# A filter-and-MLP kernel on one core: pieces 6 and 7 of the weight conversion moved to before the filter's first block, ScalarE's share of a piece one step later, and the last pieces spread over other quads

## The chip, the cores and the metric

The kernel runs on one core of a Trainium2 chip. The metric is the time on the device in microseconds (us), the median of several executions. One core has TensorE (PE in the profile; PEld is its weight load), VectorE (DVE), ScalarE (ACT), GpSimd (POOL) and SyncE (SP). Each works through its own instructions in order and waits for others by semaphores. SP does nothing here but issue DMA transfers; POOL issues others, and a few come from ScalarE.

## The reference

```
X = rfft(x, axis=1)                      # x: 8 x 3008 x 256, float32
Y = X * (filt_r + 1j * filt_i)           # filter: 1505 x 256
y = irfft(Y, n=3008, axis=1)             # 8 x 3008 x 256
h = y.reshape(24064, 256) @ w_in         # w_in: 256 x 2048
g = where(h > 0, h, exp(min(h, 0)) - 1)
out = g @ w_out                          # w_out: 2048 x 256
```

The two weight matrices arrive as float64, as pairs of 32-bit words, and the kernel turns them into float32 on the chip.

## The kernel before

**The transform.** 3008 is 47 times 64. Of each of the 8 batches, the forward transform first applies a factor of length 64 (six chunks c of four residues each, `a_first` for batch 0, `x_unit` and `a_unit` for the others) and then, in eight blocks g of the spectrum, a factor of length 47, called the second factor here (`b_unit`). `b_unit` also multiplies by the filter: eight matmuls into two PSUM tiles `psr` and `psi`, then four DVE instructions (L309 to L312). `bi_unit` takes the block back through the length 47 (matmuls into `pva` and `pvb`, two copies on ACT, L329 and L330), `y_write` puts it into DRAM, `y_read` reads it back in another layout, and `n_unit` applies the last factor (matmuls L360, two copies L362, four adds of DVE L383 to L386 that prepare the operands of the product with `w_in`). In what follows B(g) is `b_unit` of batch 0 and block g, and I(g) is `bi_unit` of the same.

**The MLP.** Its work is a list of items (batch b, sixth m of the rows, quarter q of the 2048 columns), 192 in all. One step i of the loop at the end of the kernel is called a quad here: it issues the product with `w_in` of item i ("up") and the product with `w_out` of item i-1 ("down"). Both are done as seven matrix products of half size with sums before and after them (Strassen's scheme in Winograd's form), each product being four matmuls of PE: L408 for up, into PSUM tiles phs, pha and phd, L490 for down, into po. ACT copies up results (L419) and computes the exponential part in two instructions (L425, L426), DVE adds (L416), joins (L430) and forms the sums for the way down (L466 to L470). phs is one tile that three copies read in turn, so PE's next matmuls into it wait for the copy before. Item 0 has no way down beside it, so in quad 0 PE has up work alone.

**The order of the work** is written by hand: each engine executes its instructions as they are issued in the program. In a quad it is

```
for k in "UUDUDDU": ...          # four up products, three down products
for fn, a in plan.get((i, 0)):   # place 0 of quad i
for k in "DUUDUDD": ...          # the other three up and four down products
up_tail(); down_tail()
for fn, a in plan.get((i, 1)):   # place 1 of quad i
```

`plan` holds the rest of the work, put there with `at(quad, place, function, arguments)`: the transform of the next batch, loads, outputs. In quads 0 to 3 this includes the conversion of the last weight piece, `x_unit` and `a_unit` of batch 1, and (quad 1, place 1) `n_unit(0, 1)`.

**The weight conversion.** A piece k (0 to 15, four to each quarter q: two of `w_in`, two of `w_out`) is 128 by 512 numbers. `w_fetch(k)` loads it (512 KB, one transfer for a piece of `w_in`, two for one of `w_out`; L564). `w_split` is two DVE instructions on the upper word (L576, L577: mantissa and exponent). `w_float` is four instructions of ACT (L582: lower word to float; L583: mantissa to float; L586 and L587: exponent to a power of two). `w_join` is DVE again (L593, L595, then L600 or two of L606). After each second piece `w_sums` adds four DVE instructions (L614 to L617) that form the sums of the weights. `step(k)` in the program is split and float of piece k and then the join of piece k-1. There are two sets of temporary tiles, used by even and odd pieces in turn.

**The opening phase**, before the quads: SP's queue carries x, the transform's tables and some pieces; POOL's queue carries the first pieces, then rearranges the filter in DRAM (`f_arrange`, L623 to L636, into `fd`), then reads it in eight blocks (`f_read`, L292, into `ff`), with pieces 10 to 15 in between and behind. A fetch needs its buffer: pieces 6 to 9 are loaded into the buffers of the x chunks 0 to 3 once `a_first` has read them. `a_first(c)` is 16 matmuls (L250) in two halves with eight copies by ACT (L257); `x_load_first(c)` loads its rows in two transfers (L238, L239) and, for c = 2 and 4, the table of two chunks (L243). `t_first(g)` transposes block g on PE (L269) and copies it with ACT (L270, two per block) into a tile whose buffer, for blocks 6 and 7, is that of blocks 4 and 5, so that this copy waits for the matmuls of B(4) and B(5). B(g) uses the same two PSUM tiles for every g from 1 on, and I(g) the other two: B(g+1) on PE waits for the product g on DVE, and I(g+1) for the copies of I(g) on ACT.

In the phase of the second factor, step g of the loop issues `t_first(g + 2)` (g from 2 to 5), I(g-2), B(g), the write of block g-2, and then, for g below 6, `step(g + 6)`: pieces 6 to 11 are converted there, pieces 0 to 5 before it, 12 to 14 after it, and 15 in quads 0 to 2.

Of the kernel before, what the change touches and what calls it, by code (L numbers as in the profile page):

```python
# [33 lines left out]
NXC = H // XC  # L34
# [79 lines left out]
def kernel(  # L114
# [9 lines left out]
    nc = tc.nc  # L124
# [446 lines left out]
    def w_split(k):  # L571
        m, e, c = wtmp[k % 2 if k < 15 else 0]
        f, l = c[:, 0], c[:, 1]
        wts[k] = m, e, f, l
        hi = wds[k][:, :, 1]
        nc.vector.tensor_scalar(out=m, in0=hi, scalar1=0x000FFFFF, scalar2=None, op0=ALU.bitwise_and)  # L576
        nc.vector.tensor_scalar(out=e, in0=hi, scalar1=0x7FF00000, scalar2=None, op0=ALU.bitwise_and)  # L577

    def w_float(k):
        m, e, f, l = wts[k]  # L580

        nc.scalar.activation(out=l, in_=wds[k][:, :, 0], func=AXT.Identity, scale=2.0 ** -52)  # L582
        nc.scalar.activation(out=f, in_=m, func=AXT.Identity, scale=2.0 ** -20, bias=1.0)  # L583

        ef = e.bitcast(FP32)
        nc.scalar.activation(out=ef, in_=e, func=AXT.Relu, scale=-8.0, bias=edges[:, 0:1])  # L586
        nc.scalar.activation(out=e, in_=ef, func=AXT.Relu, scale=-1.0, bias=edges[:, 1:2])  # L587
# [50 lines left out]
    with tc.manual_schedule():  # L638


        with tc.tile_pool(name="boot", bufs=1) as bp:
            ff = bp.tile([P, NG, 2, 2, D], FP32, name="ff")
            once = bp.tile([P, 2, P], FP32, name="once")
            eye, gf = once[:, 0], once[:, 1].rearrange("p (v q) -> p v q", v=2)
            pq = [bp.tile([P, 2, D], FP32, name="pq%d" % i) for i in range(2)]
            zt[0] += [bp.tile([P, 16 * ROWS], FP32, name="zt%d" % i) for i in range(2)]

            for z in zt[0] + zt[1]:
                nc.gpsimd.memset(z.rearrange("p (k r) -> p k r", r=ROWS)[:, :, 48:64], 0.0)
            for k in (1, 2, 3):  # L650
                w_fetch(k)
            f_arrange()
            w_fetch(0, nc.sync)
            for c in range(NXC):
                x_place_first(c)
            for c in range(3):
                x_load_first(c)
            w_fetch(4, nc.sync)
            nc.scalar.memzero(ff[:, 0:NG // 2])
            nc.vector.memset(ff[:, NG // 2:NG], 0.0)  # L660
            wtmp.append([kp.tile([P, 512], U32, tag=t, name=n) for t, n in (("k0", "wm"), ("k1", "we"))] +
                        [kp.tile([P, 2, 512], FP32, tag="c", name="wfl")])
            wtmp.append([sdp.tile([P, 2, D], FP32, tag="sd", name=n).bitcast(U32).rearrange("p a b -> p (a b)")
                         for n in ("wm", "we")] +
                        [t1p.tile([P, XC, D], FP32, tag="t1", name="wfl").rearrange("p (a b) d -> p a (b d)", a=2)])
            for i, v in enumerate((1151.0 * 2 ** 23, 255.0 * 2 ** 23)):
                nc.vector.memset(edges[:, i:i + 1], v)

            def step(k):
                w_split(k)  # L670
                w_float(k)
                if k > 0:
                    w_join(k - 1)

            for k in range(3):
                step(k)
            w_fetch(5, nc.sync)
            for c in range(3, NXC):
                x_load_first(c)
            nc.sync.dma_start(once, once_d)  # L680
            nc.sync.dma_start(gs, gs_d)
            a_first(0)
            w_fetch(6, nc.sync)
            step(3)
            for c in (1, 2):
                a_first(c)
                w_fetch(c + 6, nc.sync)
            step(4)
            a_first(3)
            w_fetch(9, nc.sync)  # L690
            step(5)
            for c in (4, 5):
                a_first(c)
            tn_read(0, 0)
            for g in range(NG):
                f_read(0, g, ff[:, g])
                if 3 <= g < 5:
                    w_fetch(g + 7)
            for k in (12, 13):
                w_fetch(k)  # L700
            for g in range(4):
                t_first(g)
            for g in range(NG + 2):
                if 2 <= g < NG - 2:
                    t_first(g + 2)
                if g >= 2:
                    bi_unit(0, g - 2)
                if g < NG:
                    b_unit(0, g, ff[:, g], gf, pq if g % 2 else None)
                if g >= 2:  # L710
                    y_write(0, g - 2, (nc.sync, nc.scalar if g == NG + 1 else nc.sync))
                if g < 6:
                    step(g + 6)
                    if g == 0:
                        w_fetch(14)
                if g == 7:
                    w_join(11)
                    w_split(12)
            w_float(12)
            y_read(0, 0, (nc.sync, nc.scalar))  # L720
            step(13)
            w_fetch(15)
            step(14)
        w_join(14)
        for c in range(2):
            x_load(1, c)
        yp = pool("yp", 2)
        gp = pool("gp", 2)
        ep = pool("ep", 2)
        op = pool("op", 1)  # L730
        n_unit(0, 0)

        PER = 24
        plan = {}

        def at(quad, place, fn, *a):
            plan.setdefault((quad, place), []).append((fn, a))


        for quad, place, fn in ((0, 0, w_split), (0, 1, w_float), (1, 1, w_join), (2, 1, w_sums)):
            at(quad, place, fn, 15)
        for c in range(2, XBUFS):
            at(c - 2, 0, x_load, 1, c)
        for i, f in enumerate(fbufs):
            at(3 + i, 1, nc.vector.memset, f, 0.0)
        for b in range(B):
            t = (b - 1) * PER
            if b > 0:  # L750
                for c, s in enumerate((1 if b == 1 else 0, 2, 3, 4, 6, 7)):
                    at(t + s - 1, 0, x_unit, b, c)
                    at(t + s, 0, a_unit, b, c)
                    nb, nxt = (b, c + XBUFS) if c + XBUFS < NXC else (b + 1, c + XBUFS - NXC)
                    if nb < B:
                        at(t + s, 0, x_load, nb, nxt)
                    at(t + s, 0, z_write, b, c)
                for g in range(NG + 2):
                    s = t + 9 + g
                    if g >= 2:  # L760
                        at(s, 1, bi_unit, b, g - 2)
                    if g < NG:
                        at(s, 1, b_unit, b, g)
                    if g >= 2:
                        at(s, 1, y_write, b, g - 2)
                for g in range(NG):
                    s = t + 7 + g
                    at(s, 1, f_read, b, g)
                    at(s, 1, z_read, b, g)
            for m, (s, place) in enumerate(((20, 0), (25, 1), (29, 1), (32, 0), (36, 0), (40, 0))):  # L770
                if b > 0 or m > 0:
                    at(t + s - (1 if m == 0 else 2), 0, tn_read, b, m)
                    at(t + s - (1 if m == 0 else 2), 0, y_read, b, m)
                    at(t + s, place, n_unit, b, m)
                at(t + PER + 4 * m + 5, 0, c_unit, b, m)
                at(t + PER + 4 * m + 6, 0, o_unit, b, m)

        items = [(b, m, q) for b in range(B) for m in range(6) for q in range(4)]
        for i in range(-PER, len(items) + 3):
            ups, up_tail = up_steps(*items[i]) if 0 <= i < len(items) else ((), None)  # L780
            downs, down_tail = down_steps(*items[i - 1]) if 1 <= i <= len(items) else ((), None)
            ups, downs = list(ups), list(downs)
            for k in "UUDUDDU":
                s = ups if k == "U" else downs
                if s:
                    s.pop(0)()
            for fn, a in plan.get((i, 0), ()):
                fn(*a)
            for k in "DUUDUDD":
                s = ups if k == "U" else downs  # L790
                if s:
                    s.pop(0)()
            if up_tail:
                up_tail()
            if down_tail:
                down_tail()
            for fn, a in plan.get((i, 1), ()):
                fn(*a)
# [32 lines left out]
```

## Time and profile before

| | us |
|---|---|
| median of 6 runs | 2655.39 |
| fastest and slowest of them | 2653.61, 2656.33 |
| the profiled execution's own time | 2656.33 |
| its span, first to last instruction | 2654.5 |
| busy: PE, DVE, ACT, POOL | 2601.7, 1843.8, 1509.1, 236.8 |
| first matmul of a quad (L408) | 106.71 |
| first product with the filter on DVE (L309) | 49.61 |

The mean granted clock of TensorE is 0.990 of full speed. Of the chain of work that ended last, followed back from the last instruction, 97% is PE, 43% of the span in the down products of L490. In rows of a timeline the first number is the start in us from the beginning of the span, the second the duration (or, where several are merged, the time from the first start to the last end), and in brackets at the end stands the time that the engine was idle before the instruction and what released it. DMA shares are the mean busy share of the core's 16 DMA engines. An issue row of SP or POOL is only the time to put a transfer into its queue, not the transfer.

### The profile page before, as it was taken

The page shows a single profiled execution, that of the slowest core. Times are in us where ns is not written, and L with a number is a line of the kernel's source. Part 1 is how long each engine was busy: PE and PEld are TensorE (multiplying, and loading weights), DVE is VectorE, ACT ScalarE, POOL GpSimd, SP SyncE. Part 2 cuts the span into 40 slices and gives each one's busy share as a digit, 9 for nine tenths or more (in the row PEclk, how much of TensorE's full clock was granted, in tenths as well). Part 3 has the DMA queues.
Part 4 walks back from the last instruction along what each step waited for, and adds up shares of the span by engine and source line. Part 5 has one row for each costly group of instructions (what it writes and reads, how often), then busy time and mean ns, then how long its engine had stood idle before and what let it go on. Part 6 is the DMA issues. An engine that isn't in the chain of part 4 may idle for free.

```text
span 2654.5 us, 37333 instructions
## 1 busy us (share of the span) xinstructions
PE 2601.7 (98%) x13508; PEld 2215.6 (83%) x13508; DVE 1843.8 (69%) x3203; ACT 1509.1 (57%) x2622; POOL 236.8 (9%) x298
## 2 busy tenths in 40 slices
PE   5799999999999999999999999999999999999998
PEld 4488789887898878988789878898789887899887
DVE  5776766677666776667767676676767677666666
ACT  6655555555555555655556555565555655555554
POOL 5001200011000210002100021001210011000000
PEclk8899999999999999999999999999999999999999
DMA  9534311533134322333214342134321333110010
GB/s 281 137 89 106 97 39 43 119 89 86 33 80 109 75 76 50 95 75 93 69 38 103 80 105 61 39 88 106 96 53 39 76 81 85 38 40 19 21 28 17
DMA packets 224456, 202.85 MB, mean 76 GB/s; under 512 B 127586, under 2 KB 191090, under 8 KB 224272
## 3 DMA queue, kind: packets, MB, share of 16 engines
q1 hardware_dynamic: 211632, 166.70, 25.3%
q0 software_dynamic: 11184, 33.04, 4.9%
q8 instruction: 107, 1.75, 0.3%
q10 hardware_dynamic: 1456, 0.72, 0.1%
q14 instruction: 77, 0.63, 0.1%
HBM read 128.52 MB, written 74.97 MB: 77 GB/s over the span
## 4 chain that ended last, share of the span: by engine, by line
PE 97%; DMA 2%; DVE 1%; ACT 0%; issue 0%; SPq 0%; POOL 0%; DVEq 0%; ACTq 0%; POOLq 0%
PE po L490 43%; PE phs L408 25%; PE phd L408 12%; PE pha L408 6%; PE psn L360 3%; PE pva L297 2%; PE psr L297 2%; PE psa L209 2%; DMA xc<-in_x_dram 1%; PE psa L250 0%; PE pvb L297 0%; DMA ff<-fd 0%; DMA f<-in_moe_w_out_dram 0%; PE po L269 0%; PE psi L297 0%
## 5 line engine op out<-in xcount | busy, mean ns | idle before, releaser
L490 PE MATMUL po<-g,wo 128*128 128x256 f32 (+1 forms) x5376 | 1298.2, 376 | 0.0
L490 PEld LDWEIGHTS po<-g,wo 128*128 128x128 f32 x5376 | 1016.2, 190 | 129.8 <-issue 15.8
L419 ACT ACTIVATE g<-phs 128x512 f32<-128x512 f32 (+1 forms) x576 | 339.1, 589 | 846.7 <-PE phs L408 846.0
L416 DVE TENSOR_TENSOR g<-phd,g 128x512 f32<-128x512 f32 (+1 forms) x384 | 259.6, 676 | 461.6 <-ACT e L426 277.7
L426 ACT ACTIVATE e<-e 128x512 f32<-128x512 f32 (+1 forms) x768 | 477.5, 622 | 24.4
L408 PE MATMUL phs<-y,wi 128*128 128x256 f32 (+1 forms) x1536 | 395.6, 380 | 0.0
L408 PE MATMUL phs<-ys,wi 128*128 128x256 f32 (+1 forms) x1536 | 389.1, 376 | 4.0 <-ACT g L419 4.0
L430 DVE SCALAR_TENSOR_TENSOR g<-e,g 128x512 f32<-128x512 f32 (+1 forms) x576 | 387.2, 672 | 0.2 <-ACT e L426 0.2
L425 ACT ACTIVATE e<-g 128x512 f32<-128x512 f32 (+1 forms) x576 | 352.9, 613 | 32.6 <-DVE g L416 28.0
L408 PEld LDWEIGHTS phs<-y,wi 128*128 128x128 f32 x1536 | 285.1, 190 | 83.2 <-ACT t L329 34.1
L408 PEld LDWEIGHTS phs<-ys,wi 128*128 128x128 f32 x1536 | 292.6, 191 | 37.9 <-ACT g L419 4.7
L430 DVE SCALAR_TENSOR_TENSOR g<-e,phs 128x512 f32<-128x512 f32 (+1 forms) x192 | 130.0, 677 | 139.7 <-ACT e L426 139.7
L408 PE MATMUL pha<-y,wi 128*128 128x256 f32 (+1 forms) x768 | 194.2, 375 | 0.0
L425 ACT ACTIVATE e<-phs 128x512 f32<-128x512 f32 (+1 forms) x192 | 113.0, 589 | 142.3 <-PE phs L408 141.5
L408 PE MATMUL phd<-ys,wi 128*128 128x256 f32 (+1 forms) x768 | 193.8, 375 | 0.0
L408 PE MATMUL phd<-y,wi 128*128 128x256 f32 (+1 forms) x768 | 193.7, 375 | 0.0
L318 POOL TENSOR_TENSOR sr<-sr,sp 128x512 f32<-128x512 f32 x56 | 71.2, 1271 | 1246.3 <-DVE sp L311 1246.3
L408 PEld LDWEIGHTS pha<-y,wi 128*128 128x128 f32 x768 | 146.4, 191 | 16.7
L408 PEld LDWEIGHTS phd<-ys,wi 128*128 128x128 f32 x768 | 145.7, 190 | 16.7 <-DVE g L416 0.2
L408 PEld LDWEIGHTS phd<-y,wi 128*128 128x128 f32 x768 | 145.8, 190 | 16.5
L467 DVE TENSOR_TENSOR g<-g,g 128x512 f32<-128x512 f32 (+1 forms) x192 | 130.7, 681 | 6.7
L470 DVE TENSOR_TENSOR g<-g,g 128x512 f32<-128x512 f32 (+1 forms) x192 | 130.7, 681 | 6.6
(133 smaller groups left out, 2384.1 us busy)
## 6 DMA issues: line engine op xcount, KB each, us to landing
yd<-t SPq DMA_DIRECT2D x127, 192.0 KB
t<-yd SPq DMA_DIRECT2D x190, 128.0 KB
z<-t SPq DMA_DIRECT2D x84, 256.0 KB
f<-fd POOLq DMA_DIRECT2D x112, 192.0 KB, 3.6
t<-z SPq DMA_DIRECT2D x224, 96.0 KB
out_dram<-o SPq DMA_DIRECT2D x632, 32.0 KB
tn<-tn_t SPq DMA_DIRECT2D x48, 256.0 KB
xc<-in_x_dram SPq DMA_DIRECT2D x84, 128.0 KB
```

Source lines behind the costliest of these rows:

```text
L297: nc.tensor.matmul(ps[:, u:u + w, :], table[k, v, :], r[k, u:u + w, :], start=n == 0, stop=n == len(rhs) - 1)
L318: nc.gpsimd.tensor_tensor(out=sr, in0=sr, in1=p, op=ALU.add)
L360: nc.tensor.matmul(ps[:, ts(q, P)], t[:, i - 4 * m, ds(dh * P, P)], w[:, i - 4 * m, :], start=True, stop=True)
L408: nc.tensor.matmul(ps[:, a, 0:h], w_in[q][:, COMBO[n], a, :], y[n], start=start and a == 0, stop=True, skip_group_check=True)
L416: nc.vector.tensor_tensor(out=g[o], in0=i0, in1=i1, op=ALU.add)
L419: nc.scalar.activation(out=g[o], in_=i0, func=AXT.Copy)
L425: nc.scalar.activation(out=e, in_=src, func=AXT.Relu, scale=-1.0)
L426: nc.scalar.activation(out=e, in_=e, func=AXT.Exp, scale=-1.0)
L430: nc.vector.scalar_tensor_tensor(out=g[n], in0=es[n], scalar=1.0, in1=src, op0=ALU.subtract, op1=ALU.max)
L467: nc.vector.tensor_tensor(out=b12, in0=b22, in1=b12, op=ALU.subtract)
L470: nc.vector.tensor_tensor(out=g["t4"], in0=g["b21"], in1=g["t2"], op=ALU.subtract)
L490: nc.tensor.matmul(po[i][:, u, 0:h], w_out[q][:, COMBO[n], a, :], g[n][:, a, :], start=q == 0 and a == 0 and n in (1, 3, 6, 4), stop=True, ...
```

## The change

Pieces 6 and 7: `step(6)` moves from behind B(0) to before `a_first(4)`, and the split of 7 and the join of 6 to before the transposes of the first blocks. For this the fetch of piece 6 moves up on SP's queue, ahead of the rows of x chunk 5 and of the tables `once` (with the identity for the transposes) and `gs`. In the phase of the second factor, four steps remain in place of six: after B(g), for g from 0 to 3, DVE joins piece g+7 and splits piece g+8, and ACT's four instructions for piece g+7 (g from 0 to 4) are issued between I(g-2) and B(g). Piece 14 is fetched with 12 and 13; POOL's queue keeps its order. Behind the phase, piece 13 is split with 12, and the order of DVE's work on pieces 12 to 14 is the same as before but for the join of 14, which now comes after the adds of `n_unit(0, 0)`. Piece 15: split in quad 0 as before, ACT's instructions no longer behind quad 0 but two behind quad 1 and two in the middle of quad 2, the join behind quad 2 instead of quad 1, the sums in the middle of quad 3 instead of behind quad 2. The number of instructions of every kind is unchanged.

```diff
--- before.py
+++ after.py
@@ -576,11 +576,17 @@
         nc.vector.tensor_scalar(out=m, in0=hi, scalar1=0x000FFFFF, scalar2=None, op0=ALU.bitwise_and)
         nc.vector.tensor_scalar(out=e, in0=hi, scalar1=0x7FF00000, scalar2=None, op0=ALU.bitwise_and)
 
-    def w_float(k):
+    def w_float(k, part=None):
         m, e, f, l = wts[k]
+        if part == 1:
+            return w_power(e)
 
         nc.scalar.activation(out=l, in_=wds[k][:, :, 0], func=AXT.Identity, scale=2.0 ** -52)
         nc.scalar.activation(out=f, in_=m, func=AXT.Identity, scale=2.0 ** -20, bias=1.0)
+        if part is None:
+            w_power(e)
+
+    def w_power(e):
 
         ef = e.bitcast(FP32)
         nc.scalar.activation(out=ef, in_=e, func=AXT.Relu, scale=-8.0, bias=edges[:, 0:1])
@@ -675,12 +681,13 @@
             for k in range(3):
                 step(k)
             w_fetch(5, nc.sync)
-            for c in range(3, NXC):
+            for c in (3, 4):
                 x_load_first(c)
+            a_first(0)
+            w_fetch(6, nc.sync)
+            x_load_first(5)
             nc.sync.dma_start(once, once_d)
             nc.sync.dma_start(gs, gs_d)
-            a_first(0)
-            w_fetch(6, nc.sync)
             step(3)
             for c in (1, 2):
                 a_first(c)
@@ -689,6 +696,7 @@
             a_first(3)
             w_fetch(9, nc.sync)
             step(5)
+            step(6)
             for c in (4, 5):
                 a_first(c)
             tn_read(0, 0)
@@ -696,8 +704,10 @@
                 f_read(0, g, ff[:, g])
                 if 3 <= g < 5:
                     w_fetch(g + 7)
-            for k in (12, 13):
+            for k in (12, 13, 14):
                 w_fetch(k)
+            w_split(7)
+            w_join(6)
             for g in range(4):
                 t_first(g)
             for g in range(NG + 2):
@@ -705,23 +715,27 @@
                     t_first(g + 2)
                 if g >= 2:
                     bi_unit(0, g - 2)
+                if g < 5:
+                    w_float(g + 7)
                 if g < NG:
                     b_unit(0, g, ff[:, g], gf, pq if g % 2 else None)
                 if g >= 2:
                     y_write(0, g - 2, (nc.sync, nc.scalar if g == NG + 1 else nc.sync))
-                if g < 6:
-                    step(g + 6)
-                    if g == 0:
-                        w_fetch(14)
+                if g < 4:
+                    w_join(g + 7)
+                    w_split(g + 8)
                 if g == 7:
                     w_join(11)
                     w_split(12)
+                    w_split(13)
             w_float(12)
             y_read(0, 0, (nc.sync, nc.scalar))
-            step(13)
+            w_float(13)
+            w_join(12)
             w_fetch(15)
-            step(14)
-        w_join(14)
+            w_split(14)
+            w_join(13)
+            w_float(14)
         for c in range(2):
             x_load(1, c)
         yp = pool("yp", 2)
@@ -729,6 +743,7 @@
         ep = pool("ep", 2)
         op = pool("op", 1)
         n_unit(0, 0)
+        w_join(14)
 
 
 
@@ -739,8 +754,9 @@
             plan.setdefault((quad, place), []).append((fn, a))
 
 
-        for quad, place, fn in ((0, 0, w_split), (0, 1, w_float), (1, 1, w_join), (2, 1, w_sums)):
-            at(quad, place, fn, 15)
+        for quad, place, fn, *a in ((0, 0, w_split, 15), (1, 1, w_float, 15, 0), (2, 0, w_float, 15, 1), (2, 1, w_join, 15),
+                                    (3, 0, w_sums, 15)):
+            at(quad, place, fn, *a)
         for c in range(2, XBUFS):
             at(c - 2, 0, x_load, 1, c)
         for i, f in enumerate(fbufs):
```

## The prediction

> **What bounds the kernel now.** First the busy time of each engine by stretch (columns: the stretch, then busy us and instruction count of PE, PEld, DVE, ACT, POOL, then granted clock, DMA share, GB/s).
>
> ```profile
> 120.00:125.00 5.00, 4.74 (x13) 4.30 (x14) 1.91 (x3) 0.75 (x2) 0.00 (x0) 0.50 0.00 1
> 125.00:130.00 5.00, 5.00 (x34) 3.93 (x33) 0.61 (x2) 2.56 (x5) 0.00 (x0) 0.86 0.19 56
> 130.00:230.00 100.00, 100.00 (x560) 88.95 (x559) 73.02 (x132) 59.48 (x105) 2.58 (x5) 1.00 0.42 104
> 230.00:2630.00 2400.00, 2400.00 (x12417) 2053.75 (x12415) 1672.93 (x2885) 1362.93 (x2363) 198.93 (x225) 1.00 0.28 69
> ```
>
> From 130 us on PE is busy for all of 100 and all of 2400 us at clock 1.00: nothing there can be hidden or uncovered unless PE stands still, and whatever PE starts earlier ends earlier, one for one. So the change is worth what it does to the first 126 us, plus any new hole in PE. There are two places.
>
> The first is the opening phase. The VectorE and SyncE timelines (start, duration, engine, line, tiles, then idle time before and its releaser):
>
> ```profile
> 32.44 0.69 DVE L600 TENSOR_TENSOR wi<-wfl,we 128x512 f32<-128x512 f32 x1
> 49.61 0.69 DVE L309 TENSOR_TENSOR sr<-psr,ff 128x512 f32<-128x512 f32 x1 [16.47 <-PE po L269]
> ```
> ```profile
> 24.33 0.48 SPq L238 DMA_DIRECT2D x<-in_x_dram  x1
> 26.05 0.61 SPq L239 DMA_DIRECT2D x<-in_x_dram  x1
> ...
> 31.46 5.26 SPq L564 DMA_DIRECT2D wd<-in_moe_w_out_dram  x4
> 37.77 1.60 SPq L564 DMA_DIRECT2D wd<-in_moe_w_in_dram  x2
> 39.41 0.42 SPq L342 DMA_DIRECT2D tn<-tn_t  x1
> ```
>
> DVE stands 16.47 us until the first filter block `ff` is in. The fetch of piece 6 (first of the four at 31.46) is issued so late because SP's transfers use eight semaphores in turn: each issue waits until the transfer eight before it has landed. So a landing is read off as the issue eight places later: x rows of chunk 3 are issued at 17.86 and let 31.46 go; chunk 4's table lets the fourth go at 36.4; chunk 5's two halves landed at 37.8 and 39.0. From 49.61 DVE works without a gap until 84.9. Then:
>
> ```profile
> 79.86 0.68 DVE L309 TENSOR_TENSOR sr<-psr,ff 128x512 f32<-128x512 f32 x1
> 86.23 0.69 DVE L309 TENSOR_TENSOR sr<-psr,ff 128x512 f32<-128x512 f32 x1 [1.22 <-PE psi L297]
> 89.98 0.69 DVE L309 TENSOR_TENSOR sr<-psr,ff 128x512 f32<-128x512 f32 x1 [1.26 <-PE psi L297]
> ```
> ```profile
> 72.28 0.72 ACT L587 ACTIVATE we<-we,edges 128x512 uint32<-128x512 f32 x1
> 72.91 1.06 ACT L270 ACTIVATE t<-po 112x512 f32<-112x512 f32 x2
> 73.87 0.60 ACT L329 ACTIVATE t<-pva 128x512 f32<-128x512 f32 x1
> 79.58 1.08 ACT L270 ACTIVATE t<-po 112x512 f32<-112x512 f32 x2 [1.58 <-PE psi L297]
> ```
>
> B(5), the product with filter block 5 (L309 on), begins when DVE is free; B(6) and B(7) wait for PE. ACT's copy of the transposes (72.91, L270) stands behind the conversion that ends there, and PE's next inverse unit I(3), at 74.52, waited 1.63 us for the copy L329 behind it.
>
> The second place is the start of the main loop:
>
> ```profile
> 116.76 0.58 ACT L426 ACTIVATE e<-e 128x448 f32<-128x448 f32 x1
> 117.24 0.65 ACT L582 ACTIVATE wfl<-f 128x512 f32<-128x512 uint32 x1
> ...
> 119.06 0.72 ACT L587 ACTIVATE we<-we,edges 128x512 uint32<-128x512 f32 x1
> 119.68 0.53 ACT L419 ACTIVATE g<-phs 128x448 f32<-128x448 f32 x1
> ```
> ```profile
> 116.00 0.92 PE L490 MATMUL po<-g,wo 128*128 128x224 f32 x4
> 120.26 1.86 PE L408 MATMUL phs<-ys,wi 128*128 128x224 f32 x4 [3.34 <-ACT g L419]
> ```
>
> Piece 15's conversion (four rows from 117.24) sits between quad 0's last exponential and quad 1's first copy (119.68). PE waits 3.34 us for that copy, the clock falls in the gap, and 120 to 125 runs at 0.50.
>
> **The change part by part.**
>
> *Main loop: conversion of piece 15 out of quad 0.* The copy follows 117.24 at once: 0.54 us, then PE at about 117.85 instead of 120.26, **-2.4**. The gap left is 116.92 to 117.85, 0.93 us. In the old run the four groups from 120.26 to 126.47 took 6.21 us; at the full rate (L408 groups start 0.76 apart from 111.92 on) they take 4 x 0.76 = 3.0. If the clock stays up that is another **-3.2**, sum -5.6. Does it? Read at half-us stretches, the clock changed at 58.1, 64.8, 75.2, 78.5, 82.0, 85.3, 99.0, 109.3, 119.5, 126.2: all multiples of 3.4 us apart. Windows with 1.65 and 1.7 us of idle PE (72.9 to 74.5, 79.5 to 81.2) dropped it; the one from 47.8 to 51.2, with 1.4, did not. 0.93 is under both. Bounds of this term: 0 and -3.2; I take all of it. [...]
>
> What the moved rows then cost: two rows of ACT (1.1 us) at the end of quad 1 stand before the copies of `y` (old 133.99 and 134.88); the second and quad 2's first copy (135.64) slip 0.1, and PE needs that at 136.96: nothing. The other two (1.46 us) in the middle of quad 2 push `e` by 0.45 and quad 3's first copy from 147.46 to about 147.7; PE needs it done at 148.77: nothing. DVE's join of piece 15 (2.0, row sum 135.80 to 137.80) and its sums (1.6) move one quad on, where DVE had idled 1.59 and 1.86 us: nothing, and with the cover gone, 1.46 + 2.0 + 1.6 = 5.1. The join of piece 14 now stands after the four adds of the first block on DVE (107.92); the add for b11 slips from 109.77 to 111.1, its reader on ACT is due at 112.56 anyway: nothing; behind it the x sums slip to 113.7 and the next add by 0.8, whose reader starts at 114.83: nothing.
>
> *Two pieces ahead.* A step on DVE is 0.66 for the split, 1.94 for the join (70.56 to 73.16), 1.6 for sums: 4.31 + 2.60 = 6.9 us leave the phase after 49.61, and 2.5 us of ACT for each piece. But the first four products keep their old spacing: each still has a join and a split behind it (after the change pieces 7 to 10 joined, 8 to 11 split), with the sums at products 0 and 2 as before. With ScalarE a step behind, each conversion (2.0 us from split to end) lies under the next product (2.4). So B(4) comes as before, and only then DVE has nothing between products. B(5) then waits for PE: B(4)'s matmuls end 1.3 after B(3), ACT is now free, two copies and one more take 1.5, I(3) starts at 73.4 instead of 74.52. I(3) with the matmuls of B(5) took 5.0 at half clock (74.52 to 79.56), 3.5 at full (I(5) from 85.84 to 88.29, the rest of B(7)'s from 88.86 to 89.95): B(5) at 76.9 to 78.4. From B(5)'s matmuls to B(6) is 6.7 (79.56 to 86.23), at full clock 1.5 less: B(6) at 82.1 to 85.1 instead of 86.23, **-1.1 to -4.1**, middle -2.5. After it the tail (two inverse units, write, read back) is unchanged.
>
> *What the reordered queue costs.* Piece 6's two halves take the places of chunk 5's rows and land at 37.8 and 39.0. Chunk 5's 512 KB follow at the 1.4 us per 256 KB of the neighbours: 41.8. PE now does chunk 5 right behind chunk 4 (36.57 to 42.52 together); chunk 4 ends near 40.0, so chunk 5 starts 1.8 late and, with 1.8 idle, probably cold: 3.4 us to 45.2, a copy, then 32 transposes (3.6 us, 43.07 to 46.64 before) at half speed until the clock's window ends near 47.8, so to 50.2, and 1.8 us of B(0)'s matmuls: 52.0. With the clock up it is 41.8 + 1.8 + 0.3 + 3.6 + 1.8 = 49.3. Before, they were ready near 48.5 and `ff` came at 49.6. B(0) is late by 0 to 2.4; I take **+1.3**, nearer neither end, since half the window positions give each. Piece 6's conversion on ACT (39.0 to 41.6) stands before chunk 4's copies, eight copies of 0.28 after it end before chunk 5's matmuls: hidden. Piece 7's fetches keep their places and land by 46; its split and the join of 6 (2.6) end by 49. POOL's queue keeps its order: pieces 12, 13, 14 followed each other before too.
>
> **Sum.** -5.6 - 2.5 + 1.3 = -6.8 on the profiled 2656.33 (span 2654.5): **2649.5**. The median, 2655.39, is 0.9 less; the profiled run is the slowest of six, so its clock windows may have lain unluckily. I keep 2649.5 for the median too.
>
> **Rivals.**
> *The clock falls all the same* (the window catches the 0.63 us at 110.4 or another hole): -3.6, 2652.7. For it: 1.65 was enough twice; against: 0.93.
> *The opening gains in full*: chunk 5 in time, B(6) 4.1 earlier: 2656.3 - 5.6 - 4.1 = 2646.6. For it: PE's holes before I(3) shrink; against: DMA share above 1.0 from 5 to 65 us leaves no room to land early.
> *Slower: quads 1 to 3 open holes.* Conversion (1.1 + 1.46), join and sums (2.0 + 1.6), 6.2 in all, come where the x sums and products of the next batch already are. If none is hidden and three holes each drop the clock for one window (1.7 lost of 3.4), that is +11.3; with the chunk late by the whole 2.4 (+1.1 more), -6.8 + 12.4 = +5.6: 2661.9. It turns against the change once more than 6.8 of it shows. Against it: the idle rows named.
> *It changes nothing*: quad 1 waits for something else at 118 and the opening stays at PE's pace: 2655.4. Against it: D groups' inputs were done by 119.6 at the latest.
>
> **How the numbers follow.** The forecast's own spread is 2648 to 2652. Forecast 0.50 (0.35 below 2650.1, 0.15 above), clock falls 0.17, full opening 0.14, holes 0.12 (0.05 within, 0.07 beyond), nothing 0.07. Faster by over 0.2% (5.3 us, about what a measurement of this kernel can tell from no change): 0.35 + 0.14 = 0.49; same: 0.15 + 0.17 + 0.05 + 0.07 = 0.44; slower 0.07. The range runs from the full opening, less a little, to 2655.5 and leaves out the holes and some of the low edge.
>
> **What would show it.** Right: PE idle about 0.9 before quad 1's second group, clock 1.00 through that quad; DVE with rows of L576 and the join between 39 and 49; B(5) and B(6) earlier; PE full from then on. Wrong: `x` landing after 42 with B(0) past 52; a clock of 0.50 after quad 0; PE idle in quads 2 or 3.

## The result, and the profile after

| | before | after |
|---|---|---|
| median (runs), us | 2655.1 (36) | 2647.83 (16) |
| fastest and slowest | 2652.04, 2658.2 | 2644.17, 2650.14 |
| the profiled execution's own time | 2656.33 | 2646.91 |
| its span | 2654.5 | 2645.1 |
| mean granted clock | 0.990 | 0.993 |
| B(0), B(4), B(5), B(6) on DVE (L309) | 49.61, 73.16, 79.86, 86.23 | 51.03, 74.58, 78.32, 83.32 |
| first matmul of `n_unit(0, 0)` (L360) | 103.17 | 100.25 |
| first matmul of `x_unit` of batch 1 (psa, L209), in quad 1 | 126.47 | 117.46 |

The ratio of the times is 0.9973 [0.9966, 0.9979], 7.3 us less by the medians. The forecast was 2649.5, 1.7 above the median. The two profiled executions differ by more, 9.42, because that of before is among the slowest of its runs and that of after below its median. Two of the executions of one experiment (e5), those that were profiled, ran at a mean granted clock of 0.362 and 0.750 and took 8769.87 and 3419.29 us; its times below leave them out.

The 9.42 us can be laid out on three marks. Up to the first matmul of `n_unit` 2.92 are gained, from there to the first psa matmul 6.09 (17.21 us in place of 23.30), and from there to the end of the program 0.41 (2529.45 in place of 2529.86). That last stretch lies between 2529.09 and 2529.96 in every profile but e5's two, so all but 0.4 us of the case is decided before 126 us. The table of stretches of the kernel after (columns as in the prediction's first fence) says the same:

```profile
120.00:125.00 5.00, 5.00 (x32) 5.00 (x31) 3.87 (x7) 3.86 (x8) 0.00 (x0) 1.00 0.75 199
125.00:130.00 5.00, 5.00 (x31) 5.00 (x30) 4.79 (x11) 2.72 (x6) 0.00 (x0) 1.00 0.11 33
130.00:230.00 100.00, 100.00 (x554) 87.20 (x553) 71.16 (x127) 60.36 (x106) 2.58 (x5) 1.00 0.39 95
230.00:2630.00 2400.00, 2400.00 (x12409) 2053.86 (x12408) 1670.46 (x2879) 1362.53 (x2363) 198.95 (x225) 1.00 0.28 69
```

PE is full in all four rows. Before, 120 to 125 ran at 0.50 and 125 to 130 at 0.86.

The lines behind `w_float` are shifted in the kernel after: ACT's four instructions of a conversion are L584, L585, L592 and L593 there (L582, L583, L586 and L587 before), and a join begins with L599 (L593 before).

The opening, on DVE and on SP:

```profile
38.67 0.43 DVE L576 TENSOR_SCALAR wm<-wd 128x512 uint32<-128x512 uint32 x1 [6.43 <-DMA wd<-in_moe_w_out_dram]
...
43.10 0.43 DVE L576 TENSOR_SCALAR wm<-wd 128x512 uint32<-128x512 uint32 x1
...
51.03 0.69 DVE L309 TENSOR_TENSOR sr<-psr,ff 128x512 f32<-128x512 f32 x1 [5.18 <-PE psi L297]
```
```profile
23.76 1.62 SPq L564 DMA_DIRECT2D wd<-in_moe_w_out_dram  x2
27.95 0.48 SPq L238 DMA_DIRECT2D x<-in_x_dram  x1
28.63 0.62 SPq L239 DMA_DIRECT2D x<-in_x_dram  x1
...
33.86 1.54 SPq L564 DMA_DIRECT2D wd<-in_moe_w_out_dram  x2
36.76 2.21 SPq L564 DMA_DIRECT2D wd<-in_moe_w_in_dram  x2
```

The split of piece 6 (38.67) and that of piece 7 (43.10) now stand in the time in which DVE had been idle for 16.47 us; a 5.18 us wait before B(0) is left. On SP the two halves of piece 6 (23.76) have gone ahead of chunk 5's rows (27.95, 28.63). Then the second factor, on DVE and ACT:

```profile
74.58 0.68 DVE L309 TENSOR_TENSOR sr<-psr,ff 128x512 f32<-128x512 f32 x1
78.32 0.69 DVE L309 TENSOR_TENSOR sr<-psr,ff 128x512 f32<-128x512 f32 x1 [1.26 <-PE psi L297]
83.32 0.69 DVE L309 TENSOR_TENSOR sr<-psr,ff 128x512 f32<-128x512 f32 x1 [2.51 <-PE psi L297]
```
```profile
70.58 0.72 ACT L593 ACTIVATE we<-we,edges 128x512 uint32<-128x512 f32 x1
73.30 1.09 ACT L270 ACTIVATE t<-po 112x512 f32<-112x512 f32 x2 [2.00 <-PE psi L297]
74.28 0.60 ACT L329 ACTIVATE t<-pva 128x512 f32<-128x512 f32 x1
```

B(4) to B(5) takes 3.74 us instead of 6.70. The conversion ends at 71.30, and the copy L270 now waits 2.00 us for PE; before, it had stood right behind the conversion, and PE had waited for ACT.

The start of the main loop, on ACT and PE:

```profile
113.18 0.58 ACT L426 ACTIVATE e<-e 128x448 f32<-128x448 f32 x1
113.66 0.52 ACT L419 ACTIVATE g<-phs 128x448 f32<-128x448 f32 x1
```
```profile
107.00 1.02 PE L408 MATMUL phs<-ys,wi 128*128 128x224 f32 x4 [0.63 <-ACT g L419]
...
110.85 1.02 PE L408 MATMUL phd<-ys,wi 128*128 128x224 f32 x4 [1.16 <-DVE g L416]
...
113.22 0.92 PE L490 MATMUL po<-g,wo 128*128 128x224 f32 x4
114.24 1.02 PE L408 MATMUL phs<-ys,wi 128*128 128x224 f32 x4
```

The copy L419 follows quad 0's last exponential directly, and the group at 114.24 has no bracket: the gap that was 3.34 us is about 0.26 (the down group of 113.22, at 0.76 for four matmuls, ends near 113.98). But a new wait of 1.16 us stands at 110.85, for the DVE add L416 of 110.17. DVE reaches that add late: behind the adds of `n_unit` it has the join of piece 14 (105.58 to 107.64), the add of 107.64, the split of piece 15 and two sums of x:

```profile
105.58 0.68 DVE L599 SCALAR_TENSOR_TENSOR we<-f,we 128x512 uint32<-128x512 uint32 x1
...
110.17 0.62 DVE L416 TENSOR_TENSOR g<-phd,g 128x448 f32<-128x448 f32 x1
```

### The profile page after: what moved, and what is told of

It is laid out like the page before. It is cut to its first block, busy times and chain, and to the rows that moved or that the text cites. A ratio compares the mean times of both kernels' runs of the same rounds, so it can differ in the third digit from the quotient of the medians.

```text
span 2645.1 us, 37334 instructions
## 1 busy us (share of the span) xinstructions
PE 2595.2 (98%) x13508; PEld 2209.6 (84%) x13508; DVE 1844.1 (70%) x3203; ACT 1508.7 (57%) x2622; POOL 236.9 (9%) x298
## 4 chain that ended last, share of the span: by engine, by line
PE 96%; DMA 2%; DVE 1%; ACT 0%; POOL 0%; issue 0%; ACTq 0%; DVEq 0%; SPq 0%; POOLq 0%
PE po L490 43%; PE phs L408 25%; PE phd L408 12%; PE pha L408 6%; PE psn L360 3%; PE pva L297 2%; PE psr L297 2%; PE psa L209 2%; DMA wd<-in_moe_w_out_dram 1%; DMA fd<-in_filt_i_dram 1%; DMA fd<-in_filt_r_dram 0%; DMA ff<-fd 0%; PE pvb L297 0%; PE psi L297 0%; DMA yd<-t 0%
## 5 line engine op out<-in xcount | busy, mean ns | idle before, releaser
L419 ACT ACTIVATE g<-phs 128x512 f32<-128x512 f32 (+1 forms) x576 | 338.8, 588 | 842.7 <-PE phs L408 842.1
L416 DVE TENSOR_TENSOR g<-phd,g 128x512 f32<-128x512 f32 (+1 forms) x384 | 259.6, 676 | 457.2 <-ACT e L426 282.3
```

The lines of the kernel that those rows point to most:

```text
L416: nc.vector.tensor_tensor(out=g[o], in0=i0, in1=i1, op=ALU.add)
L419: nc.scalar.activation(out=g[o], in_=i0, func=AXT.Copy)
```

## The experiments

Each was run beside the unchanged kernel, whose median was 2654.68 (24 runs) beside e1 to e4, 2654.9 (27) beside e5 to e8 and 2654.78 (23) beside the repeats; "before beside it" means these. The means of those three sets are 2654.83, 2654.76 and 2654.66, so times of different sets are compared below. Positions are psn (first matmul of `n_unit`) and psa (first of `x_unit` in quad 1). In the diffs "..." marks lines left out.

### e1: before, with only piece 15's new places

`w_float` is divided in two as in the change.

```diff
-        for quad, place, fn in ((0, 0, w_split), (0, 1, w_float), (1, 1, w_join), (2, 1, w_sums)):
-            at(quad, place, fn, 15)
+        for quad, place, fn, *a in ((0, 0, w_split, 15), (1, 1, w_float, 15, 0), (2, 0, w_float, 15, 1), (2, 1, w_join, 15),
+                                    (3, 0, w_sums, 15)):
+            at(quad, place, fn, *a)
```

> The kernel before, with the conversion of piece 15 alone moved as in the change (ScalarE's four instructions behind quad 1 and into quad 2, join behind quad 2, sums in quad 3); the opening phase is untouched and the join of 14 stays ahead of the adds. Theory (two places pay, the gap at quad 1 the more): the wait of 3.34 us before quad 1's second group shrinks to under 1, the clock stays at 1.00 through 120 to 125; about 4.5 us off the median of 2655.1, so 2650.6. Rival A (all of the gain is this place): 2647.8. Rival B (the opening gives nearly all and the clock falls in the smaller gap too): 2653.

Measured: 2651.08 (11 runs), 3.6 below before beside it (3.9 by the means, standard error 0.6); ratio 0.9984 [0.9975, 0.9992]. PE of e1 at the start of quad 1:

```profile
117.89 0.92 PE L490 MATMUL po<-g,wo 128*128 128x224 f32 x4
119.71 1.02 PE L408 MATMUL phs<-ys,wi 128*128 128x224 f32 x4 [0.90 <-ACT g L419]
...
122.94 0.43 PE L209 MATMUL psa<-sd,ta 64*64 64x256 f32 x2
```

The gap is 0.90 us, where 0.93 was forecast; from 119.71 to psa it is 3.23 us in place of 6.21 (120.26 to 126.47), at clock 1.00. psn to psa takes 17.63 us against 23.30, so 5.67 less, where 5.6 was forecast. And nothing is paid later: PE waits nowhere after psa. The median has only 3.6 of it; e7 bears on that.

### e2: after, with piece 15 put back and the join of 14 ahead of `n_unit`

```diff
-        n_unit(0, 0)
         w_join(14)
+        n_unit(0, 0)
...
-        for quad, place, fn, *a in ((0, 0, w_split, 15), (1, 1, w_float, 15, 0), (2, 0, w_float, 15, 1), (2, 1, w_join, 15),
-                                    (3, 0, w_sums, 15)):
-            at(quad, place, fn, *a)
+        for quad, place, fn in ((0, 0, w_split), (0, 1, w_float), (1, 1, w_join), (2, 1, w_sums)):
+            at(quad, place, fn, 15)
```

> The changed kernel with piece 15 put back behind quad 0 and the join of 14 back ahead of the adds: the opening of the change alone. Theory: B(6) about 2.5 to 3 us earlier, the gap of 3.3 us before quad 1's second group and the fall of the clock as in the kernel before; 2652.4. Rival A (the opening gives nothing, the late chunk eats it): 2655. Rival B (the opening gives nearly all): 2649.

Measured: 2652.21 (11), 2.5 below before beside it (3.0 by the means, standard error 0.5); ratio 0.9989 [0.998, 0.9998]. psn is at 100.85 (2.32 earlier than before), and the old gap is back on PE:

```profile
117.75 1.83 PE L408 MATMUL phs<-ys,wi 128*128 128x224 f32 x4 [3.34 <-ACT g L419]
119.37 2.60 PE L490 MATMUL po<-g,wo 128*128 128x224 f32 x8
...
122.66 0.43 PE L209 MATMUL psa<-sd,ta 64*64 64x256 f32 x2
```

3.34 us again, and again four matmuls take 1.83 us at the lower clock (0.50). But from 117.75 to psa it is 4.91 us here, against 6.21 before: the clock fell at 117.8 and was up again at 121.2, 3.4 us later, where before it fell at 119.5 and came up at 126.4, 6.8 us later. The same gap costs 1.3 us less at another place in the windows. The two parts add up: 3.6 + 2.5 = 6.1, against 6.7 for both together in e3, beside the same runs of before (by the means 3.9 + 3.0 = 6.9 against 6.8).

### e3: after, with the join of 14 ahead of `n_unit`

```diff
-        n_unit(0, 0)
         w_join(14)
+        n_unit(0, 0)
```

> The changed kernel with the join of piece 14 back ahead of the adds of the first block on VectorE. The changed kernel shows PE waiting 1.16 us in quad 0 for the add L416, which stands behind that join. Theory (the join's new place costs about a us, the prediction's nothing was wrong): that wait goes, the adds come some 1 us later and PE waits up to 0.8 for them; 2647.2 against 2647.8. Rival (the wait is made up by the later end of quad 0's exponentials): same within 0.3, PE idle in quad 0 moved, not removed.

Measured: 2647.96 (8), ratio 0.9973 [0.9962, 0.9983]: the kernel after. PE of e3:

```profile
107.44 0.99 PE L408 MATMUL phs<-ys,wi 128*128 128x224 f32 x4 [0.26 <-DVE ys L385]
109.07 1.02 PE L408 MATMUL phs<-ys,wi 128*128 128x224 f32 x4 [0.63 <-ACT g L419]
...
115.83 1.02 PE L408 MATMUL phs<-ys,wi 128*128 128x224 f32 x4 [0.90 <-ACT g L419]
```

The wait of 1.16 is gone, but a wait for the adds of `n_unit` (0.26) and the 0.90 us gap of e1 are there in its place. Together with the 0.63 that all have it is 1.79 us against 2.05, and psn to psa is 17.55 against 17.21 and 17.08 in two profiles of after. The theory that the new wait costs 0.6 us is not confirmed; the rival, that a wait only changes place here, fits.

### e4: after, with the join of 14 and the split of 15 at the end of quad 0

```diff
         n_unit(0, 0)
-        w_join(14)
...
-        for quad, place, fn, *a in ((0, 0, w_split, 15), (1, 1, w_float, 15, 0), ...
+        for quad, place, fn, *a in ((0, 1, w_join, 14), (0, 1, w_split, 15), (1, 1, w_float, 15, 0), ...
```

> The changed kernel with the join of 14 and the split of 15 both behind quad 0 instead of ahead of and in it. Theory: VectorE reaches L416 early, PE's 1.16 us wait in quad 0 goes and nothing takes its place, since VectorE has 2.4 us idle in quad 1: 2646.6. Rival (the next wait stands right behind: quad 1's first copy on ScalarE): PE idle before quad 1's second group grows from 0.1 to about 1.2 and the time stays at 2647.8.

Measured: 2645.44 (5), ratio 0.9964 [0.9951, 0.9976]. The 1.16 us wait is gone, and the 0.90 us one stands at quad 1's second group (114.46). psn to psa is 16.96. It was repeated beside the kernel after:

> The kernel of e4 once more beside the changed kernel. From the profiles (psn to the first psa of quad 1: 16.96 us against 17.21) only some 0.3 to 0.6 us are to be gained: 2647.3. If its first median was no chance: 2645.4.

> The changed kernel once more beside the others of this call, for more times on the same chip: 2647.8. If its place among them is other than in the first call, the differences of 1 to 2 us between the versions are not resolved.

Measured: 2645.62 (6), ratio 0.9969 [0.9958, 0.9981], and 2648.46 (11), 0.9978 [0.997, 0.9987], for the kernel after. Over both sets of runs the means are 2646.16 and 2647.98, 1.8 less with a standard error of 0.6. The profiles don't show where: psn to psa is 16.96 and 17.70 against 17.21 and 17.08. Only 0.3 us of it can be placed: the span behind psa is 2527.3 in both profiles of e4, 2527.6 and 2527.7 in those of after. So to keep the join of 14 and the split of 15 out of quad 0 is worth something; where most of it comes from, and which of the two brings it, isn't shown.

### e5: after, with ScalarE's part back beside VectorE's

```diff
             w_join(6)
+            w_float(7)
...
-                if g < 5:
-                    w_float(g + 7)
...
-                    w_join(g + 7)
-                    w_split(g + 8)
+                    step(g + 8)
```

> The changed kernel with ScalarE's part of pieces 8 to 11 back behind the product (split, conversion, join of the piece before, as in the kernel before); two pieces stay ahead. Theory: the copy of block 6's transposes again stands behind a conversion that can only start when the product 3 is done, so I(3) and B(5) come 1.1 to 1.5 us later, and the time is 2649.1. Rival (the step's lag is worth nothing, only the two pieces count): 2647.8, B(4) to B(5) still 3.7.

> The kernel of e5 once more, for a profile of an undisturbed execution and more times. Theory: from the start of B(4) to that of B(5) more than 5 us, as the copy L270 of block 6 stands behind a conversion that ends late, against 3.74 in the changed kernel; 2649.9. Rival: 3.7 and a later loss elsewhere.

Measured, 20 runs: median 2650.93, mean 2650.76, which is 2.8 us above the mean of after (2647.98; standard error 0.5) and beside e1's 2651.08. So the two pieces ahead, without the lag, bring nothing that shows beside e1: the opening's gain needs the lag. Whether the lag would bring it without the two pieces ahead was not run; and the edit also changes the order on DVE, where the split goes ahead of the join again. The place, in the second profile (PE's clock is at most 0.75 there, so its lengths are not compared), on ACT and DVE:

```profile
71.92 0.63 ACT L585 ACTIVATE wfl<-wm 128x512 f32<-128x512 uint32 x1 [2.46 <-DVE wm L576]
72.46 0.71 ACT L592 ACTIVATE we<-we,edges 128x512 f32<-128x512 uint32 x1
73.20 0.72 ACT L593 ACTIVATE we<-we,edges 128x512 uint32<-128x512 f32 x1
73.90 1.08 ACT L270 ACTIVATE t<-po 112x512 f32<-112x512 f32 x2
74.88 0.60 ACT L329 ACTIVATE t<-pva 128x512 f32<-128x512 f32 x1
```
```profile
74.14 0.68 DVE L309 TENSOR_TENSOR sr<-psr,ff 128x512 f32<-128x512 f32 x1
...
79.68 0.69 DVE L309 TENSOR_TENSOR sr<-psr,ff 128x512 f32<-128x512 f32 x1 [3.06 <-PE psi L297]
```

The conversion first waits 2.46 us for the split, which DVE reaches only after its four products; the copy L270 then follows L593 without a wait of its own, as in the kernel before. In the kernel after the same copy waited for PE. B(4) to B(5) is 5.54 us, where more than 5 was forecast (3.74 in after, 6.70 before); how much of the 1.8 us more is PE's low clock can't be told from this profile.

### e6: after, with chunk 5's rows and the two tables back ahead of piece 6

```diff
-            a_first(0)
-            w_fetch(6, nc.sync)
             x_load_first(5)
             nc.sync.dma_start(once, once_d)
             nc.sync.dma_start(gs, gs_d)
+            a_first(0)
+            w_fetch(6, nc.sync)
```

> The changed kernel with SP's queue as before the change (rows of chunk 5, once and gs ahead of piece 6), the conversion of piece 6 still ahead of chunk 4's copies. Theory: piece 6 lands near 43, ScalarE holds chunk 4's and 5's copies until 46, and B(0) is at 52 or later; 2649.5. Rival (the late chunk 5 was the greater loss, so the old queue gains): B(0) at 49.6, 2646.5.

Measured: 2649.08 (11), ratio 0.9978 [0.9969, 0.9987]; mean 2649.38, 1.4 above after (standard error 0.5). ACT of e6:

```profile
41.85 0.70 ACT L584 ACTIVATE wfl<-wd 128x512 f32<-128x512 uint32 x1 [4.55 <-DMA wd<-in_moe_w_out_dram]
...
43.72 0.72 ACT L593 ACTIVATE we<-we,edges 128x512 uint32<-128x512 f32 x1
44.35 0.36 ACT L257 ACTIVATE zt<-psa 128x256 f32<-128x256 f32 x1
```

With the old queue piece 6 comes at 41.85 (38.68 in after), and as its conversion stands ahead of the copies of chunk 4, these start at 44.35 (41.14). The transposes start at 45.91 (43.59) and B(0) at 53.97 (51.03). So with `step(6)` at its new place the reordered queue is worth 1.4 us; the old one delays B(0), by 2.9 us in this pair of profiles.

### e7: before, with work for PE in quad 1's gap

```diff
-            for k in "UUDUDDU":
+            for n, k in enumerate("UUDUDDU"):
...
+                if i == 1 and n == 2:
+                    for _ in range(7):
+                        nc.tensor.matmul(po_of[0, 0][3][:, 1, 0:224], w_in[0][:, 0, 0, :], ys[0, 0][1],
+                                         start=True, stop=True, skip_group_check=True)
```

> The kernel before with seven products of w_in and y (14 matmuls, 2.65 us) added on PE between quad 1's first down product and its second group, into a part of po3 that nothing uses; they add work and change no other result. They fill the 3.34 us gap and end before the copy that PE waits for. Theory (the fall of the clock in the gap costs time of its own): the clock stays at 1.00, the four groups to the first psa take 3.0 us instead of up to 6.2; over executions, with the window at random, 2 us: 2653.1. Rival (the gap costs only its length): 2655.1.

These matmuls (14 rows on PE) add work whose result nobody reads; the conversion of piece 15 stays in quad 0. Measured: 2653.1 (11), ratio 0.9991 [0.9982, 1.0], 1.8 below before beside it; by the means 2.2, with a standard error of 0.6. PE of e7:

```profile
117.63 2.81 PE L789 MATMUL po<-y,wi 128*128 128x224 f32 x14
121.16 1.02 PE L408 MATMUL phs<-ys,wi 128*128 128x224 f32 x4 [0.71 <-ACT g L419]
...
123.53 0.92 PE L408 MATMUL phs<-ys,wi 128*128 128x224 f32 x4
124.38 0.43 PE L209 MATMUL psa<-sd,ta 64*64 64x256 f32 x2
```

The real group still starts when the copy is done, 4.28 us after the down group at 116.88 (4.26 before, 116.00 to 120.26), but the idle time ahead of it is 0.71, and from it to psa it is 3.22 us against 6.21, at clock 1.00 (from 115 to 125 us) where before has 0.50. PE does more work and the kernel is faster: the fall of the clock after the gap has a price of its own, 3.0 us in this pair of profiles and about 2 over the executions.

### e8: e4, with work for PE before the first `n_unit`

```diff
+        fill = psO.tile([P, 2, 256], FP32, name="po3")
+        for _ in range(17):
+            nc.tensor.matmul(fill[:, 0, :], w_in[0][:, 0, 0, :], gs.rearrange("p a b c -> p (a b c)")[:, 0:256],
+                             start=True, stop=True, skip_group_check=True)
         n_unit(0, 0)
```

> The kernel e4 (join of 14 and split of 15 behind quad 0) with 17 products of a table added on PE between the last inverse unit and the first n_unit, about 7.3 us of the 8.6 us that PE waits for the read back; their result is used nowhere. Theory: the clock is up when psn starts, its 16 matmuls take 1.9 instead of 3.7 us, quad 0's first groups run at full rate: 2 us off e4, 2643.5. Rival (quad 0 is bound by the copies and adds behind psn, so its speed is no use): 2645.4. Rival B (the added matmuls run into psn): above 2646.

> The kernel of e8 once more beside e4 and the changed kernel. From the profiles (psn to psa 15.20 against 16.96): 1.8 us below e4 and 2 to 2.4 below the changed kernel. Rival: no difference to e4.

Here too nobody reads what is added. In e4 PE stands idle for 8.7 us ahead of the first `n_unit`, which then runs at half clock (0.50 from 95 to 100 us, 0.53 from 100 to 105; e8 has 1.00 in both). PE of e4, then of e8:

```profile
100.73 3.75 PE L360 MATMUL psn<-tn,t 128*128 128x128 f32 x16 [8.68 <-ACT wfl L585]
```
```profile
98.56 2.02 PE L360 MATMUL psn<-tn,t 128*128 128x128 f32 x16 [1.57 <-DMA t<-yd]
```

The unit's sixteen matmuls take 2.02 us instead of 3.75 (they begin as the read `t<-yd` lands), and psn to psa is 15.20 (15.61 in the repeat). Measured: 2644.76 (5), ratio 0.9962 [0.995, 0.9975], and 2645.57 (6), 0.9968 [0.9956, 0.998]; the mean of both is 2645.31, 0.85 below e4 with a standard error of 0.8, so unresolved (in the second set the two medians, 2645.57 and 2645.62, don't differ), and 2.7 (0.6) below after. It has the lowest mean of all that were tried, but the 2 us that the theory gave these matmuls over e4 are not shown.

## Why the prediction was right, and where it was not

| term | forecast | the pair of profiles | alone, over the executions |
|---|---|---|---|
| main loop, psn to psa (gap and clock) | -5.6 | -6.09 | -3.6 (e1) |
| opening (B(6) earlier, B(0) later) | -2.5 + 1.3 = -1.2 | -2.92 | -2.5 (e2) |
| the rest, behind psa | 0 | -0.41 | |
| sum | -6.8 | -9.42 | -6.1; both together -7.3 (after) and -6.7 (e3) |

The forecast laid its -6.8 on the profiled 2656.33, which is 1.2 above the median of before; that is most of the 1.7 us by which 2649.5 lies above the result. The pair's -6.09 is made up of -3.2 for the gap, -3.0 for the clock behind it, +1.3 with the new wait in quad 0, and -1.1 that is chance: ahead of quad 0's fourth group (111.06 before, 107.00 after) the clock came up 3.5 us behind psn, at 103.7, and not 6.1 behind it, at 109.3.

**The gap**: -2.4, measured 3.34 - 0.90 = 2.44 in e1. Right.

**The clock**: -3.2 taken, the far end of the bounds. In the profiles of before and e1 it is nearly right: 6.21 - 3.23 = 2.98. (The 3.0 of the working took the groups as 0.76 us apart; the rows from 111.92 on are 0.76 to 0.91 apart.) Over the executions it is 1.2 (e1's 3.6 less 2.44) to 1.8 (e7) by the medians, 1.5 to 2.2 by the means. The step that failed is that one execution's position of the windows stood for all. In the twelve profiles outside e5 the clock changes at points that lie multiples of about 3.4 us apart, at another offset in each, and e2's profile shows the same gap of 3.34 us with 3.4 us of half clock where before has 6.8. That this is the whole reason is not shown in the unprofiled executions.

**Moved rows of piece 15: nothing.** Right: PE is full from 115 us on, and the rest after psa is constant. The rival of holes in quads 1 to 3 is refuted by e1 too.

**Join of 14: nothing.** Wrong in the row, right in the sum. The working compared with readers at 112.56 and 114.83, times of an execution whose clock came up at 109.3. In the one after it came up at 103.7, PE was earlier than those times, and waited 1.16 us. e3 shows that this takes the place of another wait; e4, that with the split of 15 moved too 1.8 us can be had.

**Spacing of the products.** B(0) to B(4) was forecast unchanged: 23.55 us in both. From B(6) to psn, forecast unchanged, it is 16.94 and 16.93. B(0) to B(6) fell by 4.33 (36.62 to 32.29), at the far end of -1.1 to -4.1 and not at the middle of -2.5: the clock stayed up from 66.5 to 93.0, where it had changed four times. In all eight profiles with the new opening and queue it is 32.3 to 34.9 (mean 33.2), in three with the old one 36.3 to 38.4 (mean 37.1). So the mechanism held, and -2.5 was too small a size. It needs the lag (e5), as the working had it with its conversion that lies under the next product.

**B(0) late by 1.3.** In the pair it is 1.42, by the route described: chunk 5 starts at 41.11 (41.8 forecast) after 2.11 us of waiting for `x`, its matmuls take 2.69 (between 1.8 and 3.4), the transposes end at 48.6. But over the profiles of eight executions with the new queue B(0) lies at 47.76 to 51.03, mean 49.6, and of three with the old opening at 49.0 to 49.68, mean 49.4; in three of the eight (e2, e3, e4) DVE's wait there ends with the load of `ff`, so that the late chunk doesn't count. The term is about 0.2, not 1.3, with a standard error of some 0.4 from so few profiles: again one execution stood for all.

So the forecast holds with a right mechanism in each large part and two errors in size that offset: about 2 too much for the clock in quad 1 and about 1.3 too little for the opening. That they offset is luck. By the number alone the rival "the opening gains in full" (2646.6) was a little nearer; alone the opening gave 2.5 to 3.0, between the forecast's 1.2 and that rival's 4.1.

## What to carry to other kernels

Ask of each in-order engine what stands right ahead of the instruction that the bounding engine waits for: taking ACT's conversions off that place, once by a quad (e1) and once by one step of a pipeline (e5), is what the gain rests on, and no work was removed. Price the clock as an expected value over the positions of its windows, with the profile's value as an end of the range. Before moving work into time that is idle in a profile, ask whether the same change moves that time: here the readers came earlier because of the change itself.

## What the runs showed of the hardware

As far as stretches of half a microsecond tell, the points at which the granted clock changed lay multiples of about 3.4 us apart in each of the twelve profiles outside e5, at another offset in each execution. Cut into windows at those points, from 18 to 135 us, they hold 238 windows of full clock: after all 36 with more than 1.8 us of idle PE the clock fell, after 13 of 15 with 1.6 to 1.8, after 2 of 20 with 1.0 to 1.6, and after none of 167 with less. So a gap of 3.34 us, of which one window always has at least 1.67, should nearly always drop the clock (an estimate); what its place decides is for how long. Matmuls that nobody reads, put into idle PE time, made the kernel faster by about 2 us (e7). The runs of a single kernel spread over some 4 to 6 us (after: 2644.17 to 2650.14), while the 2529 us behind the first psa varied by less than 0.9 over the profiles: in these, what differs lies ahead of it.
